# Experts as seven products of quarters, weights stationary in both layers, results turned back

## The chip, the core and the metric

The kernel runs on one core of a Trainium2 chip. A core has TensorE (PE: matmuls, with its weight loads as PEld), VectorE (DVE), ScalarE (ACT), GpSimd (POOL) and SyncE (SP), each with its own instruction queue, and 16 DMA engines. The metric is the device time of one execution in microseconds; the median over the runs is compared.

## The reference

A chunked attention feeds a mixture of experts that gives each token to one expert. What matters here is the second part:

```python
N, D, E, F = (3072, 512, 8, 1024)
logits = x @ w_gate
expert_idx = np.argmax(logits, axis=1)
gate_w = probs[np.arange(N), expert_idx]
...
for e in range(E):
    lo, hi = (boundaries[e], boundaries[e + 1])
    h = np.maximum(x_sorted[lo:hi] @ w1[e], 0.0)
    y_sorted[lo:hi] = h @ w2[e]
y = y_sorted[inv_perm]
return (gate_w[:, None] * y).astype(np.float32)
```

All is in float32. `x` is the attention's output: batch 4, 8 heads of 64, 768 positions, so 3072 tokens of 512. Worked out with the reference's inputs, the experts get 529, 195, 426, 381, 565, 320, 162 and 494 tokens.

## The kernel before

**Attention and routing.** The tokens go through the attention in 32 blocks of 96 (`scores`, `values`, `turn_q`, `turn_k`, `turn_xb`, `logits`). After each group of blocks the routing (`routed`) finds each token's expert and place, and POOL scatters the token's row of 528 numbers (512 of x, the token's number, its gate) into `x_dram`, where each expert has room for `XC` rows. SP issues all loads in program order: q, k, v of the blocks (`load_q`, `load_k`, `load_v`), and from block 16 on one piece per block of the weights of experts 0 and 1 (`fetch_w(0, 4)`, `fetch_w(1, 4)`, pieces of 512 KB, `fetch_piece`).

**Early rows.** Up to 256 tokens of expert 0 that came in the first 22 blocks are gathered early, and their two layers run on PE while the last blocks are routed (`early_rows`, lines 970 and 984). Expert 0 has 273 tokens left after these.

**An expert.** Its tokens are gathered from `x_dram` into `xe`, 128 tokens to a group with the tokens on the partitions (`fetch_x`, one indirect DMA by POOL for each of `NG = XC // 128` groups, line 860). There are two buffers of `xe` and two of the weights: when expert e is through, the weights of expert e + 2 are loaded by SP and its rows gathered by POOL. `turn_x` turns a group on PE into PSUM (four 128x128 transposes, line 1111) and VectorE copies it into `xT` (line 1106), features on the partitions. `first_layer` keeps a 128x128 block of w1 stationary and moves the tokens: 4 matmuls for each of 8 blocks f of the hidden features (line 1117), then a relu on VectorE from PSUM into `h` (line 1104). `second_layer` keeps 128 tokens' `h` stationary and moves w2, 512 columns: 8 matmuls per group of 128 tokens or of the rest (line 1130). That gives rows of tokens at once; ScalarE scales them by the gate out of PSUM (line 1132), and POOL scatters them to `out` (`store`, line 1136).

**How many tokens.** The token counts are only known at run time. Each expert is a `tc.Switch` over the `WIDTHS` (0, 128 to 768 by 32, 832 to 1024 by 64), so every width is a program of its own, and PE, ACT, DVE and POOL branch by a register. `parts` cuts a width into pieces of 128 to 384 tokens: 288 is 128 + 160, 448 is 256 + 192, 576 is 256 + 320. The first layer's matmuls move the piece's tokens, rounded to 32 by the width; the second layer has one set of 8 matmuls per group of up to 128.

**Order.** The order on each engine is the program's (`tc.manual_schedule`); semaphores are set from the buffers that instructions share. `turn_next(e + 1)` turns the next expert's first two groups before the last second-layer group of expert e; its further groups are turned between the first-layer blocks (`todo`).

Of the kernel before, what the change touches and what calls it, by code (L numbers as in the profile page):

```python
# [10 lines left out]
F32 = mybir.dt.float32  # L11
BF16 = mybir.dt.bfloat16
I32 = mybir.dt.int32
AX_X = mybir.AxisListType.X
OP = mybir.AluOpType
AF = mybir.ActivationFunctionType
PSUM = bass.MemoryType.PSUM
DRAM = bass.MemoryType.DRAM

B, H, S, D = 4, 8, 768, 64  # L20
NMEM = 8
CHUNK, LEFT, RIGHT = 32, 16, 8
QB = 96
# [3 lines left out]
N, DM, E, F = B * S, H * D, 8, 1024  # L27
# [40 lines left out]
NV, NQ = 6, 2  # L68
PAIRS = QB
NSB = NB // 2  # L70
XC = 1024
DX = 528
SKIP = 4096
DV = 80

WIDTHS = [0] + list(range(128, 769, 32)) + list(range(832, XC + 1, 64))
CAP = 384


GROUPS = [(0, 6), (6, 12), (12, 17), (17, 22), (22, 27), (27, NB)]  # L80
# [4 lines left out]

def parts(n):

    out, o = [], 0
    while o < n:
        r = n - o  # L90
        w = r if r <= 256 or (r <= CAP and o > 0) else 128 if r <= CAP else 256
        out.append((o, w))
        o += w
    return out


def window(qb):
# [415 lines left out]
def ordinary(ctx, tc, q, k, v, mem_k, mem_v, moe_w_gate, moe_w1, moe_w2, out, good):  # L513
# [58 lines left out]
    nc.gpsimd.memset(seen[:, 0], 0.0)  # L572
    nc.gpsimd.tensor_copy(seen[0:1, 0], ebase[0:1])
    dest = cpool.tile([QB, NB], I32, name="dest")
    xr = cpool.tile([QB, NXR, DX], F32, name="xr")
    nc.gpsimd.memset(xr[:, :, DM:], 0.0)
    xe0 = cpool.tile([128, 2, DX], F32, name="xe0")
    nc.gpsimd.memset(xe0, 0.0)
# [295 lines left out]
    def count_up():  # L874

        cnt = cur["bank"][:, 4 * (D + 1) + 8 * E : 4 * (D + 1) + 9 * E + 1]
        mm(cnt[:, 0:E], lhsT=ones[0:QB], rhs=seen[:, NB], start=True, stop=True)
        mm(cnt[:, E : E + 1], lhsT=ones[0:QB], rhs=okn, start=True, stop=True)
        nc.vector.tensor_tensor(count, cnt[:, 0:E], ebase, op=OP.subtract)
        nc.vector.tensor_tensor(count[:, 0:1], count[:, 0:1], n0, op=OP.subtract)  # L880
        first = cpool.tile([128, E], F32, name="first_row")
        nc.vector.tensor_copy(first, ebase)
        nc.vector.tensor_copy(first[:, 0:1], n0)

        there = cpool.tile([128, E, NG], F32, name="there")
        nc.vector.tensor_tensor(there, bc(place, 1, E), bc(count, 2, NG), op=OP.is_lt)
        far = cpool.tile([128, E, NG], F32, name="far")
        nc.vector.tensor_tensor(far, bc(place, 1, E), bc(first, 2, NG), op=OP.add)
        nc.vector.tensor_scalar(far, far, float(-E * XC), None, op0=OP.add)
        nc.vector.tensor_tensor(far, far, there, op=OP.mult)  # L890
        nc.vector.tensor_scalar(rows, far, float(E * XC), None, op0=OP.add)
        c = cases[:, 0:E]
        part = cpool.tile([128, 2, E], I32, name="part")
        nc.vector.tensor_scalar(c, count, 31.0, None, op0=OP.add)
        nc.vector.tensor_scalar(c, c, 5, None, op0=OP.arith_shift_right)
        nc.vector.tensor_scalar(c, c, 3, 21, op0=OP.subtract, op1=OP.min)
        nc.vector.tensor_scalar(part[:, 0], count, 1.0, None, op0=OP.min)
        nc.vector.tensor_tensor(c, c, part[:, 0], op=OP.max)
        nc.vector.tensor_scalar(part[:, 1], count, 63.0 - 768.0, 0.0, op0=OP.add, op1=OP.max)
        nc.vector.tensor_scalar(part[:, 1], part[:, 1], 6, None, op0=OP.arith_shift_right)  # L900
        nc.vector.tensor_tensor(c, c, part[:, 1], op=OP.add)
        nc.vector.tensor_scalar(c, c, len(WIDTHS) - 1, None, op0=OP.min)

        most = cpool.tile([128, 2], F32, name="most")
        nc.vector.tensor_tensor(count[:, 0:1], count[:, 0:1], n0, op=OP.add)
        nc.vector.reduce_max(most[:, 0:1], count, axis=AX_X)
        nc.vector.tensor_scalar(most[:, 0:1], most[:, 0:1], float(XC), None, op0=OP.is_le)
        nc.vector.tensor_scalar(most[:, 1:2], cnt[:, E : E + 1], float(QB * 2 * NB * H), None, op0=OP.is_equal)
        nc.vector.tensor_tensor(good, most[0:1, 0:1], most[0:1, 1:2], op=OP.mult)
# [35 lines left out]
    def fetch_piece(n):  # L945
        while pieces and n:
            pieces.pop(0)()
            n -= 1
# [49 lines left out]
    with tc.manual_schedule():  # L998
# [13 lines left out]
        for i in range(NB):  # L1012
# [29 lines left out]
                    work.extend(routed(g))  # L1042
            if i == 16:
                fetch_w(0, 4)
                fetch_w(1, 4)
            if i >= 16:
                fetch_piece(1)
            if len(scatters) >= EARLY and "early" not in cur:
# [17 lines left out]
        late = logits(n - 3, banks[1])  # L1066
        values(n - 1, 1, banks[1])
        nc.vector.tensor_copy(*late)
        fetch_piece(99)
        routing(99, "v")  # L1070
        do_early(2)
# [20 lines left out]
        do_early(1)  # L1092

    actx.close()
    mpool = ctx.enter_context(tc.tile_pool(name="mpool", bufs=2))
    ps_h = ctx.enter_context(tc.tile_pool(name="ps_h", bufs=4, space=PSUM))
    ps_x = ctx.enter_context(tc.tile_pool(name="ps_x", bufs=2, space=PSUM))
    ps_y = ctx.enter_context(tc.tile_pool(name="ps_y", bufs=2, space=PSUM))

    def move(eng, out, in_, relu=False):  # L1100
        if eng is nc.scalar:
            nc.scalar.activation(out, in_, AF.Relu if relu else AF.Copy)
        elif relu:
            nc.vector.tensor_scalar(out, in_, 0.0, None, op0=OP.max)  # L1104
        else:
            nc.vector.tensor_copy(out, in_)  # L1106

    def turn_x(s, g, eng):
        tx = ps_x.tile([128, DM // 128, 128], F32, tag="x", name="txs")
        for c in range(DM // 128):  # L1110
            turn(tx[:, c], s["x"][:, g, 128 * c : 128 * c + 128], ident)  # L1111
        move(eng, s["xT"][:, :, 128 * g : 128 * g + 128], tx)

    def first_layer(s, h, o, w, f, eng):
        ph = ps_h.tile([128, CAP], F32, tag="h", name="ph")
        for c in range(DM // 128):
            mm(  # L1117
                ph[:, 0:w],
                lhsT=s["w1"][:, c, 128 * f : 128 * f + 128],
                rhs=s["xT"][:, c, o : o + w],  # L1120
                start=c == 0,
                stop=c == DM // 128 - 1,
            )
        move(eng, h[:, f, 0:w], ph[:, 0:w], relu=True)

    def second_layer(s, h, o, j, m):
        g = (o + j) // 128
        py = ps_y.tile([128, DM], F32, tag="y", name="py")
        for f in range(F // 128):
            mm(py[0:m], lhsT=h[:, f, j : j + m], rhs=s["w2"][:, f], start=f == 0, stop=f == F // 128 - 1)  # L1130
        y = s["y", g] if ("y", g) in s else mpool.tile([128, DM], F32, name="y", bufs=4)
        nc.scalar.activation(y[0:m], py[0:m], AF.Copy, scale=s["x"][0:m, g, DM + 1 : DM + 2])  # L1132
        return y, g

    def store(s, y, g, m=128):
        nc.gpsimd.indirect_dma_start(  # L1136
            out=out,
            out_offset=bass.IndirectOffsetOnAxis(ap=s["x"][0:m, g, DM : DM + 1].bitcast(I32), axis=0),
            in_=y[0:m],
            in_offset=None,  # L1140
            bounds_check=N - 1,
            oob_is_err=False,
        )

    def turn_next(e):
        if e < E:
            turn_x(ms[e], 0, nc.vector)
            turn_x(ms[e], 1, nc.vector)

    def expert(e, n):  # L1150

        s = ms[e]
        todo = list(range(2, -(-n // 128)))
        ps = parts(n)
        for k, (o, w) in enumerate(ps):
            h = mpool.tile([128, F // 128, CAP], F32, name="h")
            need = -(-(ps[k + 1][0] + ps[k + 1][1]) // 128) if k + 1 < len(ps) else 0
            for f in range(F // 128):
                first_layer(s, h, o, w, f, nc.vector)
                if f % 2 and todo and todo[0] < need:  # L1160
                    turn_x(s, todo.pop(0), nc.vector)
            for j in range(0, w, 128):
                if k + 1 == len(ps) and j + 128 >= w:
                    turn_next(e + 1)
                m = min(128, w - j)
                store(s, *second_layer(s, h, o, j, m), m)
        if n == 0:
            turn_next(e + 1)

    with tc.manual_schedule():  # L1170
        for e in range(E):
            ms[e]["xT"] = None
        for g in range(2):
            store(early, early["y", g], g)
        ms[0]["xT"] = mpool.tile([128, DM // 128, XC], F32, name="xsT")
        turn_next(0)
        xes.append(mpool.tile([128, NG, DX], F32, name="xe1", bufs=1))
        nc.gpsimd.memset(xes[1], 0.0)
        fetch_x(1)
        for e in range(E):  # L1180
            if e + 1 < E:
                ms[e + 1]["xT"] = mpool.tile([128, DM // 128, XC], F32, name="xsT")
            for a in tc.Switch(index[e], len(WIDTHS)):
                expert(e, WIDTHS[a])
            if e + 2 < E:
                fetch_w(e + 2, 1)
                fetch_piece(99)
                fetch_x(e + 2)
# [39 lines left out]
```

## Time and profile before

| | |
|---|---|
| median of 14 runs | 601.21 us (598.03 to 608.9) |
| profiled execution | 598.74 us, span of the profile 597.0 us, granted TensorE clock 0.971 |
| PE, PEld, DVE, ACT, POOL busy | 543.5, 405.9, 159.3, 109.3, 143.2 us |
| second layer of the experts, PE (line 1130) | 416 records, 182.2 us |
| first layer of the experts, PE (line 1117) | 896 records, 166.5 us |
| first matmul of the experts / end of the last | 222.8 us / 587.3 us |
| DMA | 75.77 MB, 127 GB/s in the mean |

The page lists busy times of one execution, the span in 40 slices, the chain of work that ended last (each step followed back to what released it), and groups of instructions by source line, engine, operation and tiles with their count, busy time, mean duration and the idle time before them. One float32 matmul is two MATMUL and two LDWEIGHTS records. A matmul's record is longer than its share of the array, since matmuls are pipelined; what one costs is read from start to start, as in the chain.

### The profile page before, as it was taken

To read this page: it belongs to the slowest core of one execution; us is meant where nothing else is said; L and a number is where in the kernel's file an instruction comes from. 1 tells how busy PE (TensorE), PEld (TensorE's weight loads), DVE (VectorE), ACT (ScalarE), POOL (GpSimd) and SP (SyncE) were. 2 spreads that over 40 slices of the span, in tenths; PEclk is the share of its full clock that TensorE was granted. 3 is DMA by queue.
4 is the path that set the end of the run, shared out by engine and by line. 5 is a ranking of instruction groups with operands and counts; after the bars stand their busy time and mean duration, and the time that the engine had idled before them with its cause. 6 is when DMAs were issued, how large, how long until landed. Compare 5 with 4: busy or idle time off the path is not lost.

```text
span 597.0 us, 8028 instructions
## 1 busy us (share of the span) xinstructions
PE 543.5 (91%) x2958; PEld 405.9 (68%) x2958; DVE 159.3 (27%) x488; ACT 109.3 (18%) x237; POOL 143.2 (24%) x195
## 2 busy tenths in 40 slices
PE   3799979798988989989899989989998998999993
PEld 3699969798987647757567567565653784756661
DVE  3555536354645201111111111121110111122110
ACT  2466535354542100000000000000000000000000
POOL 2000300303335366215151015005000321420100
PEclk9999969899988999999999999999999999999997
DMA  9999968999942221083920263271005507410001
GB/s 170 164 181 181 174 148 176 268 212 260 237 163 69 64 55 58 19 278 94 305 67 36 82 231 100 77 248 50 32 0 183 172 19 240 149 31 2 36 4 38
DMA packets 82144, 75.77 MB, mean 127 GB/s; under 512 B 40252, under 2 KB 65084, under 8 KB 81984
## 3 DMA queue, kind: packets, MB, share of 16 engines
q1 hardware_dynamic: 71936, 54.60, 38.7%
q0 software_dynamic: 9376, 19.30, 10.2%
q8 instruction: 47, 0.77, 0.7%
q14 instruction: 113, 0.93, 0.6%
q10 hardware_dynamic: 672, 0.18, 0.1%
HBM read 72.61 MB, written 13.04 MB: 143 GB/s over the span
## 4 chain that ended last, share of the span: by engine, by line
PE 74%; issue 10%; DMA 7%; DVE 3%; ACT 2%; another core or an unknown queue 2%; SPq 1%; POOL 0%; POOLq 0%; ACTq 0%; DVEq 0%
PE py L1130 23%; PE ph L1117 23%; PE sc L657 7%; PE o L685 6%; PE tqk L617 4%; PE o L709 3%; DMA kn<-in_k_dram 3%; PE ph L970 3%; PE py L984 2%; DMA xe<-x_dram,rows 2%; PE tx L695 2%; PE txs L1111 2%; DMA out_dram<-y,xe 2%; DVE kT L643 1%
## 5 line engine op out<-in xcount | busy, mean ns | idle before, releaser
L1130 PE MATMUL py<-w,h 128*128 128x512 f32 (+3 forms) x416 | 182.2, 593 | 0.0
L1117 PE MATMUL ph<-xsT,w 128*128 128x256 f32 (+5 forms) x896 | 166.5, 345 | 12.6 <-issue 7.2
L1117 PEld LDWEIGHTS ph<-xsT,w 128*128 128x128 f32 x896 | 148.0, 192 | 34.6 <-issue 21.2
L1130 PEld LDWEIGHTS py<-w,h 128*128 128x128 f32 (+3 forms) x416 | 73.0, 178 | 95.2 <-issue 94.1
L1104 DVE TENSOR_SCALAR h<-ph 128x256 f32<-128x256 f32 (+5 forms) x112 | 41.4, 376 | 237.6 <-PE ph L1117 219.0
L1132 ACT ACTIVATE y<-py,xe 128x512 f32<-128x512 f32 (+3 forms) x26 | 17.8, 686 | 349.2 <-PE py L1130 349.2
L1136 POOL DMA_INDIRECT out_dram<-y,xe x28 | 27.6, 987 | 220.8 <-ACT y L1132 154.3
L860 POOL DMA_INDIRECT xe<-x_dram,rows x66 | 66.5, 1008 | 27.9 <-issue 21.8
L685 PE MATMUL o<-v,ex 128*96 128x65 f32 x512 | 58.0, 257 | 4.0 <-PE tqk L617 2.0
L685 PEld LDWEIGHTS o<-v,ex 128*96 128x96 f32 x512 | 52.1, 173 | 4.9 <-issue 2.6
L657 PE MATMUL sc<-qT,kT 128*128 128x192 f32 x256 | 53.3, 356 | 1.5 <-ACT qT L625 1.5
L674 ACT ACTIVATE ex<-sc,cst 128x256 f32<-128x256 f32 x96 | 38.4, 470 | 67.2 <-PE sc L657 50.8
L657 PEld LDWEIGHTS sc<-qT,kT 128*128 128x128 f32 x256 | 45.6, 208 | 1.9 <-issue 1.4
L793 POOL DMA_INDIRECT x_dram<-xr,dest x32 | 29.7, 929 | 44.5 <-DVE inv_all L688 24.0
L643 DVE COPY kT<-tqk 64x384 f32<-64x384 f32 x64 | 35.5, 554 | 15.4 <-PE tqk L617 14.7
L1106 DVE COPY xsT<-txs 128x512 f32<-128x512 f32 x26 | 17.3, 687 | 76.8 <-PE txs L1111 62.1
L625 ACT COPY qT<-tqk 64x384 f32<-64x384 f32 x64 | 31.7, 495 | 9.1 <-PE tqk L617 8.4
L741 POOL TENSOR_TENSOR seen<-seen,onehot 96x8 f32<-96x8 f32 x32 | 6.4, 199 | 110.1 <-DVE lg L744 56.7
L688 DVE RECIPROCAL inv_all<-o 96x4 f32<-96x4 f32 x64 | 13.9, 217 | 70.3 <-PE o L685 46.8
L617 PE MATMUL tqk<-cst,kn 96*128 96x96 f32 (+1 forms) x128 | 18.1, 273 | 11.4 <-DMA kn<-in_mem_k_dram 6.1
L690 DVE TENSOR_TENSOR xr<-o,inv_all 96x256 f32<-96x256 f32 x64 | 26.9, 421 | 2.2
L695 PE MATMUL tx<-cst,xr 96*128 96x96 f32 x128 | 17.0, 256 | 9.7 <-DVE kT L647 4.4
(96 smaller groups left out, 269.7 us busy)
## 6 DMA issues: line engine op xcount, KB each, us to landing
w<-in_moe_w_dram SPq DMA_DIRECT2D x12, 2048.0 KB
w<-in_moe_w_dram SPq DMA_DIRECT2D x16, 512.0 KB
kn<-in_k_dram SPq DMA_DIRECT2D x16, 384.0 KB
qn<-in_q_dram SPq DMA_DIRECT2D x16, 384.0 KB
v<-in_v_dram SPq DMA_DIRECT2D x24, 128.0 KB
v<-in_v_dram SPq DMA_DIRECT2D x24, 112.0 KB
v<-in_v_dram SPq DMA_DIRECT2D x8, 144.0 KB
xe<-x_dram,rows POOLq DMA_INDIRECT x66
```

Source lines behind the costliest of these rows:

```text
L617: turn(tt[:, a], t[0:n, 2 * a + x], ident[0:n, 0:n])
L625: nc.scalar.copy(to[:, :, :, t], tq[D * t : D * t + D])
L643: i = nc.vector.tensor_copy(to, of[:, :, 0:PAIRS].rearrange("d a (y z p) -> d a y z p", y=2, z=2))
L657: ins = mm(o.rearrange("p (x t) -> p x t", x=2), lhsT=turned[b][:, a, w0 : w0 + WIN], rhs=sbs[i // 2]["qT"][:, a, :, QB * (i % 2) : QB * ( ...
L674: nc.scalar.activation(ex4[:, :, :, sl], sc4[:, :, :, sl], AF.Exp, bias=mask[:, 3 * x + g : 3 * x + g + 1], scale=D**-0.5)
L685: mm(o[:, j], lhsT=s["ex"][:, h], rhs=s["v"][:, h, 0 : D + 1], start=True, stop=True)
L695: turn(tx[:, c], s["x"][:, 128 * c : 128 * c + 128], ident[0:QB, 0:QB])
L793: i = nc.gpsimd.indirect_dma_start(out=x_dram, out_offset=bass.IndirectOffsetOnAxis(ap=dest[:, t : t + 1], axis=0), in_=xr[:, t % NXR].bit ...
L860: nc.gpsimd.indirect_dma_start(out=to.bitcast(I32), out_offset=None, in_=x_dram, in_offset=bass.IndirectOffsetOnAxis(ap=which, axis=0), bo ...
L1104: nc.vector.tensor_scalar(out, in_, 0.0, None, op0=OP.max)
L1117: mm(ph[:, 0:w], lhsT=s["w1"][:, c, 128 * f : 128 * f + 128], rhs=s["xT"][:, c, o : o + w], start=c == 0, stop=c == DM // 128 - 1,)
L1130: mm(py[0:m], lhsT=h[:, f, j : j + m], rhs=s["w2"][:, f], start=f == 0, stop=f == F // 128 - 1)
```

## The change

Both layers now keep the weights stationary and move the tokens, and a unit of up to 512 tokens is computed by Winograd's form of the 2x2 block product, with seven products where eight would be plain. The weights, the tokens and the result are cut into quarters (the contraction in two, the output features in two, the tokens in two halves of k). Per layer there are four token sums on VectorE (T1, T2, a difference kept in place, T4), weight sums S1, S2, S4, a fourth in place in the weights (`fresh`), and seven products of 8 matmuls with k columns each. The products go into three pairs of PSUM banks, P, Q and R, and are chained there: P holds the first, is copied out (`keep`, ScalarE, into `one`), takes the S2 T2 product on top, is copied out again, and so on to the seventh. Results are finished by VectorE sums of a PSUM bank and a kept copy, with the relu on ScalarE in place.

- S1, S2, S4 of layer one (`S1s`) are made for the next expert on POOL during layer two (`next_sums`); those of expert 0 on VectorE before it starts. Those of layer two (`S2s`) are made on VectorE in layer one.
- Units of up to 224 tokens (`DENSE`) have no quarters: `dense`, plain matmuls with the weights stationary. Widths over 512 are two units.
- The result of layer two has its features on the partitions (`yT`). `turn_y` turns each group back on PE into the PSUM tile that `turn_x` uses, ScalarE or VectorE scales it by the gate, POOL stores it. All of an expert's groups are turned and stored at its end.
- `xT`, `h` and `yT` are one buffer each. The next expert's first four groups are turned in layer two (two before the fifth product and two before the seventh) or after a dense unit, each copied by ScalarE.
- `XC` is 768 instead of 1024: six gathers per expert instead of eight, widths up to 768 only. More tokens than 768 for one expert go to the general kernel.
- Stores no longer wait for earlier stores (`declare_no_dep`).
- The weights of expert 1 are fetched after the attention's last block, as two DMAs of 2 MB, instead of in eight pieces from block 24 on. `xr` moves to a pool that is freed with the attention.

```diff
-XC = 1024
+XC = 768
-WIDTHS = [0] + list(range(128, 769, 32)) + list(range(832, XC + 1, 64))
-CAP = 384
+WIDTHS = [0] + list(range(128, XC + 1, 32))
+DENSE = 224
+UNIT = 512
 def parts(n):
-    ...
+    if n <= UNIT:
+        return [(0, n)] if n else []
+    w = -(-n // 64) * 32
+    return [(0, w), (w, n - w)]
...
             if i == 16:
                 fetch_w(0, 4)
-                fetch_w(1, 4)
...
         nc.vector.tensor_copy(*late)
+        fetch_w(1, 1)
         fetch_piece(99)
...
+    def weight_sums(eng, A, S):
+        return [
+            lambda: both(eng, S[0], A[1][0], A[1][1], add),
+            lambda: both(eng, S[1], S[0], A[0][0], less),
+            lambda: both(eng, S[2], A[0][1], S[1], less),
+        ]
+    def token_sums(B, T, n):
+        t1, t2, t4 = (t[:, :, 0:n] for t in T)
+        return [
+            lambda: both(nc.vector, t1, B[0][1], B[0][0], less),
+            lambda: both(nc.vector, t2, B[1][1], t1, less),
+            lambda: both(nc.vector, B[0][1], B[1][1], B[0][1], less),
+            lambda: both(nc.vector, t4, B[1][0], t2, less),
+        ]
+    def product(to, A, B, n, first, last):
+        rows, k = A.shape[2] // 128, A.shape[1]
+        for m in range(rows):
+            b, c = divmod(m, rows // 2)
+            for i in range(k):
+                mm(to[b][:, n * c : n * c + n], lhsT=A[:, i, 128 * m : 128 * m + 128], rhs=B[:, i], ...)
+    def layer(A, S, B, T, C, n, rows, sums_first, relu, fresh, between):
+        ...
+        def finish(to, a, b, op=add):      # VectorE, then relu on ScalarE in layer one
+        def keep(to, of):                  # ScalarE, a copy per bank
+        def first():
+            product(P, A[0][0], B[0][0], n, True, False)
+            keep(one, P)
+        def second():
+            product(R, A[0][1], B[1][0], n, True, True)
+            finish(C[0][0], R, one)
+        def fifth():
+            product(Q, S1, t1, n, True, False)
+            keep(five, Q)
+        sums[0]()
+        first()
+        if sums_first:                     # layer two
+            fifth()
+            sums[1]()
+            between(0)
+            second()
+        else:                              # layer one
+            sums[1]()
+            between(0)
+            second()
+            fifth()
+        product(P, S2, t2, n, False, False)
+        keep(one, P)
+        sums[2]()
+        if fresh:
+            both(nc.vector, A[1][0], A[0][0], A[1][0], less)
+        between(1)
+        product(Q, S4, B[1][1], n, False, True)
+        finish(C[0][1], Q, one)
+        sums[3]()
+        product(P, A[1][0], B[0][1], n, False, False)
+        finish(C[1][1], P, five)
+        between(2)
+        product(P, A[1][1], t4, n, False, True)
+        for x in range(2):
+            of = of_bank(P, rows, x, n)
+            nc.scalar.activation(C[1][0][:, c * x : c * x + c], of, AF.Relu if relu else AF.Copy)
+    def turn_y(s, g, m, eng):
+        ty = ps_x.tile([128, C1, 128], F32, tag="x", name="tys")
+        for c in range(C1):
+            turn(ty[0:m, c], yT[:, c, 128 * g : 128 * g + m], ident)
+        y = mpool.tile([128, DM], F32, name="y", bufs=4)
+        ...                                # times the gate, on eng
+        store(s, y, g, m)
```

`between` of layer one turns groups from the fifth on and makes S2s; that of layer two, in an expert's last unit, has `next_sums` before the product with A[0][1] and `turn_next(2)` before the fifth and the seventh. In layer one a product is 4 blocks of output features times 2 of the contraction, in layer two 2 times 4.

## Prediction

> **What bounds the kernel now.** First the page's busy times, then the stretch of the experts by windows, then the chain of work that ended last, then the groups by shape.
>
> ```profile
> PE 543.5 (91%) x2958; PEld 405.9 (68%) x2958; DVE 159.3 (27%) x488; ACT 109.3 (18%) x237; POOL 143.2 (24%) x195
> ```
>
> TensorE is busy in 91% of the span, nobody else in a third of it. By windows, experts 2 and 4 (columns: stretch, its length, busy time of PE, PEld, DVE, ACT, POOL, granted clock, DMA share, GB/s):
>
> ```profile
> 292.00:347.50 55.50, 53.81 (x208) 35.42 (x208) 8.92 (x20) 2.74 (x4) 12.12 (x13) 1.00 0.34 110
> 392.00:462.00 70.00, 67.95 (x228) 40.62 (x228) 10.69 (x21) 3.43 (x5) 13.13 (x14) 1.00 0.28 92
> ```
>
> PE misses some 2 us per expert at a clock of 1.00; VectorE is idle five sixths of the time. The chain has the prices (start, length, work; one fp32 matmul is two records):
>
> ```profile
> 261.89 0.69 ACT y L1132
> 262.58 1.00 issue
> 263.58 12.35 PE ph L1117 x64
> ...
> 320.94 10.40 PE ph L1117 x64
> ...
> 362.54 13.81 PE ph L1117 x64
> 376.35 6.87 PE py L1130 x16
> 383.21 0.87 PE txs L1111 x8
> ```
>
> The x64 rows are 32 matmuls of 224, 192 and 256 columns: 0.386, 0.325 and 0.432 us each, or 1.72, 1.69 and 1.69 ns per moving column. Eight matmuls of 512 columns are 6.87 us (1.68). So PE time is moving columns. A turn of 128 rows is half of 0.87, 0.44 us. The first two lines are the gap at a Switch: 1.7 us from the last matmul of one expert to the first of the next, at six of seven changes (the change at 531 us has none). By shape (count | busy us, mean ns of one):
>
> ```profile
> L1130 PE MATMUL py<-w,h 128*128 128x512 f32 x320 | 139.8, 592 | 0.0
> L1130 PE MATMUL py<-w,h 128*64 128x512 f32 x64 | 28.3, 595 | 0.0
> L1130 PE MATMUL py<-w,h 128*32 128x512 f32 x16 | 7.1, 594 | 0.0
> L690 DVE TENSOR_TENSOR xr<-o,inv_all 96x256 f32<-96x256 f32 x64 | 26.9, 421 | 2.2
> L1106 DVE COPY xsT<-txs 128x512 f32<-128x512 f32 x26 | 17.3, 687 | 76.8 <-PE txs L1111 62.1 <-PE py L1130 13.9 <-PE ph L1117 0.7
> ```
>
> In the second layer a group of 32 or 64 tokens costs as much as one of 128, for the weights move. The 26 groups take 26 x 6.87 = 178.6 us, the first layer about 163 by the same prices, turns and gaps the rest of the 364.5 us from the first expert matmul (222.8) to the last (587.3).
>
> **TensorE's work.** The counts from the inputs (273 after the early 256, then 195, 426, 381, 565, 320, 162, 494) choose the cases 288, 224, 448, 384, 576, 320, 192, 512. 224 and 192 stay dense: 64 matmuls of as many columns. 576 is two units of 288. A unit of 2k tokens is 7 products of 8 matmuls of k columns in each layer, 112k columns. At 1.69 to 1.72 ns (1.75 for k = 144, between the 192 row and the 128-column matmuls, 5.36 us for 24, 1.74): 28.2, 24.7 (dense), 43.2, 36.4, 56.4, 30.8, 20.8 (dense), 48.3 = 288.8 us. Turns: 33 of x (four per expert whatever its count, one more for 576) and 26 of y, less the four before the start, 55 x 0.44 = 24. Together 312.8.
>
> **What else lies on the path.** The switch gaps stay, 6 x 1.75 = 10.5. At an expert's end the turned results share two PSUM buffers, which empty in 0.69 us against 0.44 of turning: 0.4 to 0.6 for each of the six experts with products, 0.8 for the two dense ones, whose four x copies all queue on ScalarE: 4.2. Start: two more turns and a Switch whose gap was hidden behind the xT copy: first matmul at 224.1 instead of 222.8; then three weight sums on VectorE ahead of S1 t1: 0.5. The 1.9 us that the run of before lost in expert 6 (12.32 for 192 columns against 10.40) stay in the sum.
>
> **Waits inside a unit.** A sum of n elements on VectorE is 0.16 us + 1.03 ns x n by the 256 and 512 rows: 0.55 for 384, 0.95 for 768, 1.21 for 1024 (a weight sum). With 384 tokens a product is 2.6 us. Layer one gives VectorE four token sums, six finishing sums and four weight sums, 10.4 us beside 18.2; layer two 7.2. No matmul waits for an engine's total; it may for an order. P is evicted by ScalarE (two copies of 0.48, the price of the 384-element xT copy, 479 ns) while Q or R is multiplied. The tightest is the seventh product: it adds to P, whose first bank VectorE must have read for C11, after one finishing sum and t4: 0.1 + 3 x 0.55 = 1.75 of 2.6 us; with 288 tokens 1.5 of 2.0. Behind that wait stands all of PE's queue. Layer two starts on P at once, but bank 0 was done half a product earlier. I take nothing for these, with 0 to 0.4 a unit as range (0 to 5 in all).
>
> **POOL beside VectorE.** New on POOL are three sums of 1024 per expert for the next S1. No row has their price. POOL's fixed cost is 199 ns (8 elements), its memset 0.86 ns per element: 1.1 us if only one stream counts, 2.8 if two reads and a write go one after the other; I take 2.0, reads in turn and the write under them. They stand behind six gathers (1.3 us each) and ahead of the stores, which have four y buffers. S1 is needed two products into the next expert, over 10 us later even after the short dense ones. But:
>
> ```profile
> L918 POOL MEMSET xe<- 128x4224 f32 x1 | 3.6, 3609 | 0.0
> L776 DVE COPY xr<-tinv 96x2 f32<-96x2 f32 x1 | 3.5, 3506 | 0.0
> L776 DVE COPY xr<-tinv 96x5 f32<-96x5 f32 x3 | 0.5, 168 | 0.1
> ```
>
> A copy of two elements, 0.17 us elsewhere, took 3.5 us beside a POOL memset that began 0.1 us earlier: one engine was held for the whole of the other's instruction. POOL's sums start some 19 us into an expert (stores landing, gathers, switch) or after its fifth product, beside S2, t1, t2 and t4. If each holds back one VectorE sum for 2 us, against 0.4 to 3 us of room, about 1 us stays in each of four experts: 4 (0 if nothing is held; up to 5 x (3 x 2.0 - 2) = 20 if all three sums are lost whole, with 2 us of room).
>
> [...]
>
> **Around it.** Eight pieces of expert 1's weights (512 KB) leave SP's queue among the last v loads and follow them as two DMAs; nothing stands behind. By the timeline PE idled 0.5, 1.6, 0.4 and 2.0 us between 141 and 168, and 2.0 at 182 behind that memset, which shrinks by a quarter. I take 2.4 back (0 to 5). The end: four stores now come together at 1.3 us each (POOL's gather spacing), the last ends 4.1 after PE instead of 2.0: +2.1. Gathers fall from 66 to 50 and the choice of cases loses four VectorE operations of 0.17 us, both beside the early rows' matmuls or POOL's own: 0, and 1 us where that cover is gone.
>
> **Sum.** 224.1 + 312.8 + 10.5 + 4.2 + 0.5 + 1.9 + 4 = 558.0 for the last matmul, where before it was 587.3; + 9.7 of tail + 2.1 - 2.4 = 567.4 of span against 597.0. The profiled execution took 598.74, 1.74 over its span: 569.1. The median of the runs, 601.21, lies 2.5 above that execution, so 571.6; I say 571.
>
> **Rivals.** *The lock bites whole* (0.10): three sums lost in five experts, 571 + 16 = 587. For it: the 3.5 us copy. Against: each POOL sum waits for the one before, which lets VectorE in. *Slower* (0.07): the same lock at a higher price p, with VectorE idle while PE waits for S2 and t1. Without it I have 567.6; the 33.6 us are eaten when 5 x (3p - 2) reaches them, p = 2.9 us, just above my upper bound; at 3.5 the time is 567.6 + 42.5 = 610. *Better* (0.06): no lock, gaps hidden as at 531 us: 571 - 4 - 10 = 557. *It doesn't do what it says* (0.02): products of k columns at no less than the 256-column price per matmul, so that seven cost what eight did; the 128-column matmuls at 0.22 us speak against it; about 600, no change.
>
> **How the numbers follow.** Forecast 0.75, own range 561 to 581 (lock 0 to 10, waits 0 to 5, attention -3 to +2). To leave out 2 in 10 the range is 559 to 588. What a measurement here can tell is 0.3%, 1.8 us. Faster 0.91, same 0.02, slower 0.07.
>
> **What would show it.** Right: matmul records of 144 to 256 columns at 0.12 to 0.22 us each start to start, no py of 512; PE still over 85% busy among the experts; VectorE near 50% there; expert 4 some 64 us instead of 69.6, expert 2 some 50 instead of 55.6. Wrong: PE idle before the S1 t1, S2 t2 or last product with VectorE or POOL as releaser, over 2 us per expert; POOL sums over 2.9 us; VectorE sums of 1024 far over 1.21.

## The result and the profile after

The changed kernel takes 662.79 us (median of 10 runs) against 602.43 (47 runs): 1.100 times the time, with an interval of 1.097 to 1.103. The profiled execution took 659.25 us, its span is 657.4, its granted clock 0.899. The forecast was 571.

The page's busy times show the first surprise:

```profile
PE 529.0 (80%) x3602; PEld 499.4 (76%) x3602; DVE 243.7 (37%) x549; ACT 179.5 (27%) x406; POOL 182.2 (28%) x200
```

TensorE is busy for 14.5 us less than before, but in 80% of a longer span. The windows of experts 2 and 4, and of the stretch between experts 2 and 3 (columns as in the prediction: length, busy times of PE, PEld, DVE, ACT, POOL, clock, DMA share, GB/s):

```profile
316.00:365.40 49.40, 48.43 (x256) 47.11 (x256) 20.87 (x27) 13.32 (x27) 14.78 (x11) 0.96 0.20 63
430.97:493.72 62.75, 62.28 (x488) 61.55 (x488) 26.73 (x48) 19.64 (x50) 14.57 (x11) 0.96 0.17 55
365.39:373.96 8.57, 0.01 (x1) 0.04 (x1) 0.34 (x1) 0.69 (x1) 3.08 (x4) 0.62 0.96 326
```

Inside, the experts are what was forecast: expert 2 takes 49.4 us ("some 50"), expert 4 62.75 ("some 64"). Between them PE does nothing for 8.57 us. What PE waited for from the first expert on (total us, times, longest):

```profile
PE sum_p L1180 <- issue: 44.4, 5, 13.6
PE sum_p L1264 <- issue: 20.2, 2, 11.8
PE sum_p L1180 <- DMA out_dram<-y,xe: 4.1, 1, 4.1
PE tys L1135 <- DVE y L1142: 2.4, 6, 0.4
PE sum_p L1180 <- DVE h L1106: 2.3, 3, 1.0
PE sum_q L1180 <- DVE t L1106: 1.2, 1, 1.2
```

"issue" is waiting for nothing that the profile shows: seven times, 64.6 us, all at the Switches (11.85, 8.53, 8.57, 13.60, 8.52, 8.35, 5.17). Before, PE stood still at six of these seven changes, 1.6 to 2.0 us each. VectorE, the engine that the prediction feared, holds PE's products for 3.5 us in all. PE's timeline at the change from expert 2 to 3 (start, length; in brackets the idle time before):

```profile
364.29 1.09 PE L1135 MATMUL tys<-cst,yT 128*128 128x128 f32 x8 [0.41 <-DVE y L1142]
373.95 4.70 PE L1180 MATMUL sum_p<-xsT,w 128*128 128x192 f32 x16 [8.57 <-issue]
378.49 2.76 PE L1180 MATMUL sum_r<-xsT,w 128*128 128x192 f32 x16
381.09 2.76 PE L1180 MATMUL sum_q<-t,s 128*128 128x192 f32 x16
```

The idle costs something more behind it: the first product after it takes 4.54 us from start to start, the next 2.60 (the forecast's price). The granted clock fell while PE stood still (0.62 in the idle stretch), is 0.58 over the first product and 1.00 over the next. That costs some 2 us an idle, whatever its length: 1.6 to 2.9 us, at a granted clock of 0.50 to 0.68, behind each of the eight idles of 4.1 to 13.6 us from the first expert on. Before, five of the six idles of 1.6 to 2.0 us have no such loss; the one of 1.96 us into expert 6 has, and it is the 1.9 us that the prediction kept in its sum (12.32 against 10.40; granted clock 0.57 over the first 3.9 us).

What PE's instruction queue does in that time stands in the view of one source line. Line 1223 before and 1385 after hold the Switch's branches; the columns are count, shortest/median/longest in ns, first and last start. Before, at the same change of experts, with PE's timeline there:

```profile
L1223 PEldq COMPARE_BRANCH  x2: 320/4056/7792, 339.0 to 339.7; - x2
```

```profile
339.01 7.08 PE L1130 MATMUL py<-w,h 128*64 128x512 f32 x16
347.85 2.02 PE L1117 MATMUL ph<-xsT,w 128*128 128x128 f32 x16 [1.75 <-issue]
```

After:

```profile
L1385 PEldq COMPARE_BRANCH  x2: 407/4344/8282, 364.7 to 365.4; - x2
```

A Switch gives PE two branches: out of the case, and into the next. Here the first takes 0.3 to 0.4 us, the second about 8 us, in both kernels. The jump did not get dearer. Before, PE's queue reached it at 339.0, as the last group's eight matmuls of 512 columns began, and they ran to 346.1: of an 8.8 us jump 7.1 were covered and 1.75 bare. After, it is reached at 364.7, when only the end of one turn is left (to 365.4): 0.7 covered, 8.57 bare.

The traces do not name what a long branch waits for. Branches are of 0.3 to 0.8 us or of 3 to 9 us, and the DMA page has two queues of kind "instruction", q8 and q14, whose packets cluster at the Switches (12 of q14's between 573 and 590 us, around the last one). That the long branches wait for these packets is my reading and was not shown; what is measured is that q14 has 113 of them with the Switches and 24 without, in a3 below:

```profile
q14 instruction: 113, 0.93, 0.6%
```

```profile
q14 instruction: 24, 0.20, 0.1%
```

### The profile page after: what moved, and what is told of

The parts are those of the page before. It is cut to its first block, busy times and chain, and to the rows that moved or that the text cites. A ratio compares the mean times of both kernels' runs of the same rounds, so it can differ in the third digit from the quotient of the medians.

```text
span 657.4 us, 9731 instructions
## 1 busy us (share of the span) xinstructions
PE 529.0 (80%) x3602; PEld 499.4 (76%) x3602; DVE 243.7 (37%) x549; ACT 179.5 (27%) x406; POOL 182.2 (28%) x200
## 4 chain that ended last, share of the span: by engine, by line
PE 32%; issue 17%; DMA 11%; DVE 3%; POOLq 1%; POOL 1%; ACT 0%; another core or an unknown queue 0%; DVEq 0%; ACTq 0%
PE sum_p L1180 15%; DMA xe<-x_dram,rows 9%; PE sum_q L1180 7%; PE sum_r L1180 4%; DMA out_dram<-y,xe 2%; PE sum_r L1272 2%; PE sum_p L1264 1%; PE txs L1111 1%; DVE y L1142 1%; PE tys L1135 1%; DVE t L1106 1%; PE sum_q L1264 1%; DVE h L1106 1%; POOLq L923 1%; POOL out_dram L1120 0%
## 5 line engine op out<-in xcount | busy, mean ns | idle before, releaser
L1180 PE MATMUL sum_p<-xsT,w 128*128 128x144 f32 (+4 forms) x224 | 48.3, 382 | 48.5 <-issue 44.4
L1180 PEld LDWEIGHTS sum_p<-xsT,w 128*128 128x128 f32 x224 | 43.7, 239 | 51.4 <-issue 49.8
L1211 ACT COPY one<-sum_p 128x288 f32<-128x288 f32 (+9 forms) x56 | 21.5, 385 | 126.6 <-PE sum_p L1180 109.9
L1180 PE MATMUL sum_p<-t,w 128*128 128x144 f32 (+4 forms) x224 | 37.0, 318 | 2.4 <-DVE h L1106 2.3
L1180 PE MATMUL sum_q<-t,s 128*128 128x144 f32 (+4 forms) x224 | 36.7, 317 | 1.2 <-DVE t L1106 1.2
L1180 PEld LDWEIGHTS sum_p<-t,w 128*128 128x128 f32 x224 | 33.6, 190 | 4.3 <-DVE h L1106 3.5
L1180 PE MATMUL sum_p<-t,s 128*128 128x144 f32 (+4 forms) x224 | 36.6, 316 | 0.0
L1180 PE MATMUL sum_p<-h,w 128*128 128x144 f32 (+4 forms) x224 | 36.6, 316 | 0.0
L1180 PEld LDWEIGHTS sum_q<-t,s 128*128 128x128 f32 x224 | 34.0, 190 | 2.2 <-DVE t L1106 1.4
L1180 PEld LDWEIGHTS sum_p<-h,w 128*128 128x128 f32 x224 | 34.0, 190 | 0.8
```

The costliest lines, as they stand in the source:

```text
L1180: mm(to[b][:, n * c : n * c + n], lhsT=A[:, i, 128 * m : 128 * m + 128], rhs=B[:, i], start=first and c == 0 and i == 0, stop=last and c = ...
L1211: nc.scalar.copy(of_bank(to, rows, x, n), of_bank(of, rows, x, n))
```

## The experiments

The theory, *cover*: each Switch holds a jump of 5 to 9 us for PE; what counts is how much queued work, free of waits, stands ahead of it. Rivals: *load in the way* (the fetch of code waits behind the 2 MB of w2, which now leave before the case ends) and *lock* (POOL's sums hold VectorE). Chips differ by some 3% (the kernel before takes 582.93 us on the one of a1 and 601.91 on that of a4), so a kernel is compared with the kernel before on its own chip. The difference lies ahead of the experts: the changed kernel's first expert matmul starts at 208.5 us in a1 and at 230.5 in a4, on another chip, while eight matmuls of 192 columns take 2.60 us on both.

**Without the weight loads** (a1_few_weights).

```diff
+        if e >= 2:
+            s["w1"], s["w2"] = ms[e - 2]["w1"], ms[e - 2]["w2"]
+            for name, w in (("w1", moe_w1), ("w2", moe_w2)):
+                to, of = s[name], w[e].rearrange("(c p) f -> p c f", p=128)
+                pieces.append(lambda to=to, of=of: nc.sync.dma_start(to[:, 0:1, 0:64], of[:, 0:1, 0:64]))
+            return
```

> The changed kernel, with the two weight loads of experts 2 to 7 cut to 32 KB each (it computes those experts with the weights of expert 0 or 1, so its output is not the reference's). Theory 'cover': at each Switch PE has two branches, each of which has to fetch code; the kernel before had eight 512-column matmuls (7.0 us) queued ahead of them, the changed kernel has only the last turn (0.65 us), so that the fetch lies bare; the weight load only lengthens it. Expected: the seven PE idles at the Switches (11.85, 8.53, 8.57, 13.60, 8.52, 8.35 and 5.17 us after the change) all come near the last one, which has no load beside it, 4.5 to 5.5 us each, 36 us in all instead of 64.6; time 615 to 632 us. Theory 'load in the way' alone: the idles go back to the 1.7 to 2.0 us of before, 12 us in all, time 590 to 600 us. Theory 'lock' (VectorE held by the sums on POOL): nothing changes, 655 to 665 us.

Measured: 1.066 (1.052 to 1.079). The idles are 8.30, 4.96, 5.01, 9.04, 5.24, 9.34 and 5.08 us, 47.0 instead of 64.6. At the change from expert 2 to 3:

```profile
L1391 PEldq COMPARE_BRANCH  x2: 416/2489/4562, 335.6 to 336.4; - x2
```

The jump is 4.6 us without a load and 8 with one. So the load has a part, 17.6 us net; the rest is the bare jump. I had expected all seven near 5; in three of them the first branch too took 3.3 to 4.0 us, as it took 6.8 and 7.5 us in the two longest idles after the change. So the time missed the expectation too: 1.066 is 642 us beside a kernel before of 602, not 615 to 632. When the first branch is short and when it is long is open.

**More work behind the last turn** (a2_long_tail, and a5_half_tail with four instead of eight).

```diff
+        for _ in range(8):
+            mm(Q[0][:, 0:512], lhsT=ident, rhs=S2s[0][:, 0:2], start=True, stop=True, skip_group_check=True)
```

> The changed kernel with eight more matmuls of 512 columns (6.9 us by the row of before) behind the last turn of every expert; their result is not used. Theory 'cover': the two branches are reached while those eight run, so the bare idle at the Switches falls to 1.5 to 2.5 us each, 0 to 1 at the last, and what is added is taken off the idle; the two idles of 11.85 and 13.60 fall most, the clock is not lost, and the time is 635 to 655 us in spite of 55 us of added matmuls. Theory 'load in the way': the fetch waits for the 2 MB of w2 whatever PE does, the idles keep 5 us or more, and the time goes to 690 to 715 us. Theory 'lock': idles unchanged, 715 us.

> As a2_long_tail, with four matmuls of 512 columns behind the last turn of every expert instead of eight (3.4 us instead of 6.9). Theory 'cover': cover and bare idle add up to one jump, 9 to 9.6 us beside a weight load (0.65 + 8.53 after the change, 7.2 + 2.4 with eight); with 0.65 + 3.4 us of cover the idle is 4.8 to 5.6 us at the Switches with a load (more where the first branch has to fetch too) and 1.5 to 2.2 at the last. Theory 'load in the way': the idle doesn't follow the cover.

Measured: 1.084 (1.075 to 1.092) with eight, 1.084 (1.077 to 1.092) with four. With 55 us of useless matmuls added, the kernel is faster than without them. The idles with eight are 2.78, 1.47, 2.41, 2.21, 5.61, 2.66 and 0 us, 17.1 in all instead of 64.6 (at the one of 5.61 the first branch took 6.8 us); with four, 4.9 to 6.1 us at the six Switches with a load and 1.89 at the last. PE's timeline with eight:

```profile
339.05 7.03 PE L1335 MATMUL sum_q<-s,cst 128*128 128x512 f32 x16
348.49 2.84 PE L1180 MATMUL sum_p<-xsT,w 128*128 128x192 f32 x16 [2.41 <-issue]
```

All kernels at two changes of experts; cover is from the start of the first branch to the end of the last matmul:

| | 2 to 3: cover | idle | sum | 6 to 7 (no load): cover | idle | sum |
|---|---|---|---|---|---|---|
| before | 7.1 | 1.75 | 8.8 | 7.1 | 0 | hidden |
| after | 0.7 | 8.57 | 9.3 | 0.6 | 5.17 | 5.8 |
| a5, four more | 4.1 | 5.01 | 9.1 | 4.0 | 1.89 | 5.9 |
| a2, eight more | 7.2 | 2.41 | 9.6 | 7.2 | 0 | hidden |
| a1, no loads | 0.7 | 5.01 | 5.7 | 0.6 | 5.08 | 5.7 |

Cover and idle add up to one jump, 8.8 to 9.6 us beside a load and 5.7 to 5.9 without. *Lock* is out, and *load in the way* is a surcharge. Nor does cover grow without end in these runs: counted in the traces, 17 matmul and 16 weight load records are left to start when the first branch of a Switch begins, at all seven changes of a2 and of b1 below, and in no run here more. So eight matmuls of 512 columns (16 matmul records, 7.0 us) are about the most that was seen, and with short turns among the 17 it was less (5.3 to 5.5 us in b1). Why it is 33 was not tried.

**Without the Switch** (a3_no_switch of the changed kernel, b2_no_switch of the one before).

```diff
-            for a in tc.Switch(index[e], len(WIDTHS)):
-                expert(e, WIDTHS[a])
+            expert(e, (288, 224, 448, 384, 576, 320, 192, 512)[e])
```

> The changed kernel without the Switch: the eight experts' code in one line, with the widths that these inputs give (it is right for these counts alone). Theories 'cover' and 'load in the way': no branch, so the idles at the expert boundaries fall below 1 us, the halves of the clock behind them go too, and the time is 565 to 585 us: what the prediction summed for the products was right, and only the Switch was missing. Theory 'lock' or any other cost inside the experts: the boundaries close but the time stays over 630 us.

> The kernel before without the Switch, with the widths that these inputs give (right for these counts alone). Theory 'cover': its jumps lie behind the last group's matmuls already, so it gains only the idles that are bare, 6 x 1.75 us, and perhaps the first and last one: 0.97 to 0.985 of the kernel before, against 63 us of gain (1.100 to 0.948) that the changed kernel had from the same edit. If the jump cost the same in both kernels it would gain 60 us too, 0.90.

Measured: 0.948 (0.939 to 0.958) and 0.972 (0.967 to 0.977). The changed kernel's expert phase, from the experts' first matmul to the last, in a window of a3:

```profile
205.72:528.45 322.73, 314.29 (x2046) 303.92 (x2044) 148.44 (x202) 86.53 (x193) 129.11 (x94) 0.99 0.34 111
```

322.7 us instead of 404.5 with the Switches, PE 97% busy; on other chips the kernel before has 364.5 with them and 351.0 without. The same Switch costs one kernel 82 us and the other 13.5, and the products themselves are worth 28.

**Two short turns at the end of the kernel before** (b1_turns_last).

```diff
-                if k + 1 == len(ps) and j + 128 >= w:
-                    turn_next(e + 1)
                 m = min(128, w - j)
                 store(s, *second_layer(s, h, o, j, m), m)
+                if k + 1 == len(ps) and j + 128 >= w:
+                    turn_next(e + 1)
```

> The kernel before, with the two turns of the next expert's tokens moved from ahead of the last group's eight matmuls to behind them: no work is added, only the end of a case is now two short turns that wait for VectorE, as after the change. Theory 'cover': PE reaches the branches only at the end, the idles of 1.7 to 2.0 us become 6.5 to 8.5 us at six Switches and 0 becomes 3.5 to 5 us at the last, which has no load; with the clock the time goes from 601 to 640 to 660 us. Theory 'load in the way': the six grow (w2 is free 1.8 us before the end) but the last stays near 0. Theory 'lock': no change, 600 to 605 us.

Measured: 1.060 (1.050 to 1.070), 639 us beside 602: just short of what I expected, and not by the way that I expected. The turns found both PSUM buffers empty and waited for nobody, so PE reached the branches 5.3 to 5.5 us ahead of the end all the same (17 matmul records were left, but eight of them were short turns), and the idles at the first six Switches were 2.8 to 3.6 us, at the last none. Cover and idle are one jump again, 8.3 to 9.1 us. The rest came from another engine (PE's waits):

```profile
PE ph L1117 <- issue: 18.9, 6, 3.6
PE ph L1117 <- DVE h L1104: 9.0, 4, 2.6
```

VectorE now ends the case with the copies, jumps late itself, and its first relu is late: at the first change it stood idle for 10.1 us before it, named "issue". So VectorE has a jump of its own.

**The end of the program** (a4_eight_gathers). After the change PE's last matmul was followed by 22.4 us, before by 9.6.

```diff
-        for g in range(NG):
+        for g in (*range(NG), 4, 5):
             gather(s["x"][:, g], rows[:, e, g : g + 1])
```

> The changed kernel with two of each expert's six gathers of tokens issued twice (groups 4 and 5 again), so that the program issues 126 indirect transfers from POOL as the kernel before does, and not 110. It adds work off the path. Theory 'tail by the count of transfers': the last drain on POOL took 0.97 us before and 9.06 after, and the wait instruction ahead of it 0.39 and 2.36; in both kernels that wait grows with the number issued (1.2 us at 50, 2.4 at 110, 2.6 at 121) and is 0.39 from the 125th on, so with 126 the end gets back about 10 us: ratio to the kernel before 1.08 to 1.09 instead of 1.10, the last drain 0.97 us. Theory 'cover' alone, with the tail made by the bare jumps at the end: no change, the drain stays at 9.06 us and the ratio at 1.10.

Measured: 1.079 (1.071 to 1.087). POOL's last drain (shortest/median/longest of three), in the changed kernel and in a4:

```profile
L1385 POOLq DRAIN  x3: 44/113/9059, 647.5 to 657.1; - x3
```

```profile
L1385 POOLq DRAIN  x3: 40/113/974, 648.4 to 650.0; - x3
```

So the sixteen gathers that the change saves cost it some 10 us at the end: the end after PE's last matmul falls from 22.4 to 12.8 us when they are put back.

**A first layer by products, a second as before** (h1_products_first_layer, h2_eight_gathers with the gathers of a4; in all h kernels widths over 512 are cut into 256 and the rest).

```diff
+    def second_layer(s, o, j, m):
+        ...
+        for f in range(C2):
+            mm(py[0:m], lhsT=h[:, f, j : j + m], rhs=s["w2"][:, f], start=f == 0, stop=f == C2 - 1)
+        ...
+            for j in range(0, w, 128):
+                if final and j + 256 >= w:
+                    turn_next(4 if j + 128 >= w else 2)
+                second_layer(s, o, j, min(128, w - j))
```

> The first layer by seven products as in the change, the second as in the kernel before: h stationary, the second weights moving at 512 columns, eight matmuls per 128 tokens, no results turned back. So every case ends in eight matmuls of 512 columns (6.9 us) that wait for nothing. Theory 'cover': the idles at the Switches are 1.5 to 2.5 us again and the clock stays, though POOL still makes the next sums and the weights load as before; first layer 144 us instead of 166.5, second 182 as before; time 0.97 to 1.00 of the kernel before (the drain of 9 us at the end stays). Theory 'load in the way': w2 is free only at the case's end, idles 2 us too, same time. Theory 'lock' or 'larger code': the idles stay at 5 us or more, 1.03 to 1.08.

> The kernel h1_products_first_layer with 126 indirect transfers from POOL instead of 110, as in a4_eight_gathers. If the end of the program follows the count of transfers: about 10 us less than h1, 0.955 to 0.98 of the kernel before, faster than both kernels. If not: as h1.

Measured: 1.025 (1.020 to 1.029) and 1.011 (1.006 to 1.015), 2.5 and 3% above the upper ends of what I expected, though the idle named "issue" was nearly gone from the Switches (3.5 of the 5.2 us below are the jump into expert 0). Other waits had opened (PE's waits of h2):

```profile
PE sum_p L1171 <- POOL xe L917: 8.4, 3, 3.8
PE txs L1107 <- DMA xe<-x_dram,rows: 7.5, 4, 3.7
PE sum_p L1171 <- issue: 5.2, 4, 3.5
PE sum_p L1171 <- DVE h L1102: 3.9, 2, 3.3
```

**Mending these** (h3_vector_sums, then h4_early_engine).

> The kernel h1_products_first_layer with three mends of what its trace shows behind the closed Switches: the sums of the next expert's first weights on VectorE and not on POOL (PE waited 8.4 us for them in h2_eight_gathers, because POOL comes to them behind its own jumps, eight gathers of 1.3 us and the stores); the first expert's third and fourth group of tokens turned in its case and not ahead of its Switch (its first idle was 3.5 to 4.1 us with the branch reached late, 1.7 in the kernel before); and sixteen repeated gathers in one place, behind the Switch of expert 6, for the 8 to 10 us of the end. Theory 'cover': what is left is the sum of the products and the second layer, expert phase 343 to 352 us from the first expert's first matmul to the last (364.5 in the kernel before, 361.7 in h1), time 0.96 to 0.985 of the kernel before. If VectorE's sums or the gathers of tokens open a new wait: 0.985 to 1.01.

Measured: 1.024 (1.016 to 1.032), a miss for two reasons. The sixteen repeated gathers all wrote the same place, each waiting for the one before, and pushed the last stores back: 27 us from PE's last matmul to the end. And behind POOL's sums another wait had been hidden:

```profile
PE sum_p L1171 <- ACT one L1202: 9.4, 4, 4.1
```

ScalarE evicts the case's last result, so it jumps last and with nothing to cover it (at the change from expert 3 to 4 it stood idle for 8.7 us, named "issue", before its first copy), and its copy of the first product is due within the next three. In h4 VectorE makes that copy; `between(-1)` turns the expert's own groups from the third on, which no longer stand at the end of the case before; and the repeated gathers go over six places.

```diff
-            keep(one, P)
+            between(-1)
+            keep(one, P, nc.vector)
-        nexts = list(range(4)) if e + 1 < E else []
+        nexts = [0, 1] if e + 1 < E else []
-                run_all(weight_sums(nc.gpsimd, quarters1(e + 1), S1s))
+                run_all(weight_sums(nc.vector, quarters1(e + 1), S1s))
```

> The kernel h1_products_first_layer, mended by what h3_vector_sums showed: PE waited 9.4 us for ScalarE's first copy of a bank in the next case (ScalarE ends a case last, with the result's eviction, so that its own jump lies bare), 5.8 us for the gathers of the next tokens, and the repeated gathers, each waiting for the one before, pushed the last stores and the end back by 18 us. Here VectorE, which ends a case early, makes that first copy and the sums; only two groups of the next tokens are turned at the end of a case, the others behind the first product of their own; the sixteen repeated gathers go over six groups. Theory 'cover', for every engine: the idles behind the Switches fall below 2 us, expert phase 342 to 350 us (364.5 in the kernel before), end 9.7 us, 0.955 to 0.975 of the kernel before. If another engine's jump takes its place: 0.98 to 1.01.

Measured: 0.968 (0.963 to 0.973), faster than both kernels. Its expert phase (window):

```profile
203.02:551.29 348.27, 336.63 (x1422) 223.16 (x1421) 86.34 (x132) 63.11 (x124) 89.68 (x91) 1.00 0.34 111
```

The matmuls run from 202.52 to 550.80, half a microsecond ahead of this window: 348.3 us, and 9.9 from PE's last matmul to the end; at the change from expert 2 to 3 cover 7.0 and idle 0.82 us.

## Why the prediction was wrong

The step that failed is "The switch gaps stay, 6 x 1.75 = 10.5". It read the 1.7 us between two experts as the price of a jump. They were what was left of a jump of 8.8 us behind 7.1 us of matmuls, and the change put short turns, with waits, where those matmuls had been. The profile before held it: the branch records of line 1223, up to 8 us long, the first of each pair started 7 us before the last matmul's end, and the one gap of zero at 531 us, where no load stands beside the jump. The prediction saw that zero, made a rival of it ("gaps hidden") and did not ask what hid it.

By the prediction's sum, in us:

| | forecast | after | a3, no Switch |
|---|---|---|---|
| first expert matmul (224.1 - 2.4) | 221.7 | 230.5 | 205.7, another chip |
| idle at the Switches | 10.5 | 64.6 | 0 |
| the rest of the expert phase | 323.4 | 339.9 | 322.7 |
| end (9.7 + 2.1) | 11.8 | 22.4 | 18.7 |
| span | 567.4 | 657.4 | 547.2 |

- **PE's work: right,** and in its parts too: 323.4 forecast, 322.7 without the Switch, of which PE is busy for 314.3 (forecast for products and turns 312.8) and idle for 8.4 (10.6). The 16.5 us more with it, for which the sum has no term, are the slow first pieces behind the idles: 4.54 instead of 2.60 us as shown, and 17 us when the excess of the eight first pieces over the ones after them is added up.
- **The idle: 54 us too low**, as shown by a1, a2, a5 and a3.
- **The end: 10.6 us too low.** The four stores were not the cause; the saved gathers were (a4, with an end of 12.8 us), and the prediction counted those at nothing.
- **The start: 8.8 us late.** The jump into expert 0 lay bare for 4.1 us where 1.7 had been; the early rows' last matmul ended 3.7 us later than before instead of 2.4 earlier. That part scatters: in b2, which has the attention of the kernel before, it ended at 228.4 us, against 220.3. Whether the change moved it is not settled.
- **The lock: right in size.** POOL's sums took 2.38 to 2.54 us in the mean by kind, 3.2 at most (forecast 2.0), and VectorE was held, but PE waited 3.5 us for VectorE's sums in all, in four places, each behind a sum that was held beside POOL (1.83, 2.33, 2.45 and 2.97 us long); 4 was forecast. The timeline of expert 2 (start, length) shows a sum of 448 alone, and one that met a POOL sum:

```profile
320.76 0.62 DVE L1106 TENSOR_TENSOR t<-xsT,t 128x448 f32<-128x448 f32 x1
...
333.35 2.35 POOL L1106 TENSOR_TENSOR s<-w,s 128x1024 f32<-128x1024 f32 x1 [0.67 <-PE sum_q L1180]
...
333.85 2.33 DVE L1106 TENSOR_TENSOR t<-xsT,t 128x448 f32<-128x448 f32 x1
...
336.78 3.29 PE L1180 MATMUL sum_p<-t,w 128*128 128x224 f32 x16 [0.54 <-DVE h L1106]
```

2.33 us instead of 0.62: it ends 0.5 us after POOL's. Of the 1.7 us PE lost 0.54.
- **The rivals.** "Slower" ended on the right side by the wrong mechanism. The marks for right and wrong did their work: the products' prices held (2.60 us for eight matmuls of 192 columns), and "PE still over 85% busy among the experts" failed, with 82% (332.65 of 404.52 us). "VectorE near 50% there" was 34% (138.95 us), and 46% in a3.

## What to carry to other kernels

A gap between two pieces of a branching program can be what is left of the jump and not its price (1.75 of 8.8 us here): look up the branch's own record, and how far ahead of the last work it started. Let each engine end a case with long work that waits for nothing, and do not ask the engine that ends last for the first thing in the next case (PE waited 9.4 us for ScalarE's copies in h3). In the changed kernel the idles of 4.1 to 13.6 us cost 1.6 to 2.9 us of clock on top, whatever their length; in the kernel before five of the six of 1.6 to 2.0 us cost none.

## What was not expected of the hardware

- A branch on PE took 0.3 to 0.8 us, or 3.3 to 5.4 us, and up to 9.1 us beside a weight load of 2 MB; on VectorE, ScalarE and POOL the branch's record is short (0.04 to 0.08 us) and the time lies behind it (10.1 us of idle on VectorE in b1, 8.7 on ScalarE in h3).
- When a branch began on PE, never more than 33 records (17 matmuls, 16 weight loads) were left to start ahead of it, in every run here with a Switch.
- The wait instruction on POOL at each Switch grew with the number of indirect transfers issued, from 1.2 us after 50 to 2.6 after 121, and was 0.4 from the 124th or 125th on; the drain at the program's end took 9.06 us in the kernels with 110 transfers and 0.9 to 1.0 in those with 126. Why it falls there was not tried.
